# Column softmax turned on VectorE and through DRAM, and the last stage in written order

## Chip, cores and metric

One NeuronCore of a Trainium2 chip runs the whole program. The metric is the device time of one execution in microseconds (us). Engines are called TensorE (PE), VectorE (DVE), ScalarE (ACT), GpSimd (POOL) and the sync engine (SP), which issues nearly all DMAs.

## What is computed

Three layers, one after the other, all in float32. Every matmul of the big layers is made of three passes over a high and a low part of each operand (hi·hi, hi·lo, lo·hi), so operands are split all the time: the high part by a ScalarE copy, the low part by a VectorE subtraction.

```
# x: 8 batches, 8 heads, 512 tokens, 64;  state: 8, 8, 32 rows, 64
a     = softmax_over_rows(scale * x @ state.T)          # per token
xread = a @ state
a2    = softmax_over_tokens(scale * state @ x.T)        # per state row ("columns")
sread = a2 @ x
X = concat([xread, sread], tokens) -> 8 * (512 + 32) tokens of 512
Y = relu(X @ w1_in)**2 @ w1_out                         # 512 -> 2048 -> 512
h = Y @ w2_in                                           # 512 -> 1024
s = h * softmax(h);  ln = (s - mean) / sqrt(var + 1e-6) * g
out = ln @ w2_out                                       # 1024 -> 512
```

## The kernel before

**First layer and attention.** The list `items` holds one step for each batch b and each 128 wide chunk f of the hidden layer, 16 steps a batch; batch 8 stands for the 256 tokens read into the states (sread of all batches). A step (`step`, L1337) computes the hidden chunk f with 6 long matmuls (12 for batch 8), squares it (`square`: ScalarE relu to r, VectorE r times the PSUM bank, called r below; `high` and `low` split the square into gh and gl), and projects the chunk f-2 back to 512 columns with 12 matmuls into four accumulators (`project`). After the last chunk the accumulators are evicted to ev_x, half by ScalarE and half by VectorE, and stored (x_d). The PSUM pool of the hidden chunks has two buffers, so r of a step must be done before the hidden matmuls of the next step but one.

The attention of batch b runs spread over 15 steps (0 to 14) beside the steps of the batch before: attention step k lies in step k+2 of that batch, and 14 in step 0 of batch b itself. For batches from 2 on, `attention` returns for each k four lists: work ahead of the hidden matmuls (`tensor`), on ScalarE, on VectorE, and `after` the hidden matmuls; only the first VectorE part stands ahead of gl, and the r multiply comes after all of them. x arrives in a layout for 32x32 block turns (`load_xq`, four quarters of xbuf), is turned on VectorE in k = 0 to 3 (`turn_x`), and arrives a second time by tokens in the same buffer (`load_half`) for sread. The scores st have (4 heads x 32 rows) on partitions and 512 tokens along. The row softmax turns them on VectorE, goes over rows and turns back (`back`, k = 10 and 12). The column softmax goes along the tokens (`col_max`, `col_exp`, `col_norm`, done at k = 8 and 10), and then st must have tokens on partitions: TensorE transposes it in blocks of four into a PSUM bank (`col_ps`, L747, k = 11 and 12), ScalarE copies that to e2 (`col_copy`), and `sread` (L616) multiplies it with x in two halves of 32 small instructions, ahead of the hidden matmuls of k = 13 and 14.

**Second layer.** Tokens are taken in 17 pairs of 128-token tiles, A and B. Each pair's h comes from seven products by Strassen's scheme (`product`, 6 matmuls each, `post` for the adds on VectorE and ScalarE); product i of pair q is slot n = 7q + i (`slot`, L1433). Beside the products a slot carries the SoLU and layer norm of earlier pairs (sol_max, sol_exp, sol_mul, sol_square, sol_var with a pow on GpSimd, sol_norm), the turn of ln on VectorE and through DRAM (`turn`, `fetch_ln`), its split (`part_hi`, `part_lo` to lh and ll), the load, sums and splits of later pairs (`load_pair`, `sums` on GpSimd, `pair_hi`, `pair_lo`), and a number of steps ("flows", 3 matmuls each, 272 in all) of the down projection `down`, which takes ll and lh of one tile after the other. The last pair is turned on TensorE (`by_pe`). Slots 0 to 11 lie in steps 5 to 15 of batch 8, slot 12 and 13 between the last projections. `prepare` (L1167) loads and splits the second layer's weights in the steps of batches 7 and 8, and the first two pairs.

**What sets the order.** Engines run their queues in order. Inside `tc.manual_schedule` the order on TensorE, VectorE, ScalarE and SP is as the code writes it; GpSimd's is always planned. Up to step 28 a table of hand (PLAN) is walked through, then written steps run to the end of batch 6. From batch 7 on to slot 13 a planner with its own costs orders the instructions, and from slot 14 on the order is written again:

```
    for s in range(steady.stop, len(items)):      # batches 7 and 8: planned
        ...prepare(b, f); step(s, b, f); slots 0 to 11
    ...split_down(2); slot(12, 0); ...split_down(3); slot(13, 0)
    with tc.manual_schedule(engines=by_hand):
        for n in range(14, 7 * NPAIR):
            slot(n, {14: 0, 15: 2, 16: 1, 17: 1}.get(n, 2 if n < 32 else (2, 3, 2, 2, 3, 2, 2)[n % 7]))
        for n in range(7 * NPAIR, 7 * NPAIR + 14):
            slot(n, 3)
```

Of the kernel before, what the change touches and what calls it, by code (L numbers as in the profile page):

```python
# [20 lines left out]
def memory_attention_relu2_solu(  # L21
# [16 lines left out]
    P = 128  # L38
# [29 lines left out]
    ]  # L68
    x2p_d = [dram.tile([P, NM, S], F32, name=f"x2p_d{b}", tag=f"x2p_{b}") for b in range(2)]
# [433 lines left out]
    def attention(b):  # L503
# [111 lines left out]

        def sread(half):  # L616
# [137 lines left out]

        def col_max(q):
# [16 lines left out]
        def at(f, *a):  # L772
# [4 lines left out]
            11: [(col_ps, 0)], 12: [(col_ps, 1)], 13: [(sread, 0)], 14: [(sread, 1), (sread_out,)],  # L777
# [12 lines left out]
            11: [(a_high, 0), (col_copy, 0)],  # L790
# [18 lines left out]
        after = {12: [(col_copy, 1)]}  # L809
# [357 lines left out]
    def prepare(b, f):  # L1167
# [27 lines left out]
        elif f == 4:  # L1195
            split_block("T2", "T2", *halves_of(w_tile("w2")))
            pair_hi(0, 1)
            pair_lo(0, 1)
        elif f == 5:
            minus("T4", "R21", "T2", "R11")  # L1200
            load_pair(1)
        elif f == 6:
            split_block("B21", "R21", *halves_of(w_tile("w2")))
            pair_hi(1, 0)
            pair_lo(1, 0)
        elif f == 7:
            sums(1)
# [6 lines left out]
        if f in (12, 14):  # L1214
            split_down(f // 2 - 6)
# [121 lines left out]
    def step(s, b, f):  # L1337
# [65 lines left out]
        rest()  # L1403
        squares.append((b, f, n, r, True))
# [11 lines left out]
        if ws == 15 and 1 <= w < B - 2:  # L1416
            load_xq(w + 2, 0)
# [14 lines left out]

    def slot(n, flows):  # L1433
        q, i = divmod(n, 7)
        work = []

        def at(p, f, *a):
            if 0 <= p < NPAIR:
                work.append(lambda: f(p, *a))

        last = NPAIR - 1
        if i == 0:
            if q == 2:
                at(0, part_hi, "A")
                at(0, part_lo, "A")
            at(q - 1, sol_exp, "B")
            at(q - 1, sol_mul, "A")
        elif i == 1:
            at(q - 1, sol_square, "A")
            if 0 < q - 2 != last:  # L1450
                at(q - 2, part_hi, "A")
            at(q - 1, sol_mul, "B")
        elif i == 2:
# [4 lines left out]
            if 0 < q - 2 != last:  # L1458
                at(q - 2, part_lo, "A")
        elif i == 3:  # L1460
            at(q - 1, sol_norm, "A")
            at(q - 1, sol_var, "B")
        elif i == 4:
            at(q - 1, sol_norm, "B")
            if q - 2 != last:
# [3 lines left out]
        elif i == 5:  # L1469
            if q - 1 < last:  # L1470
                at(q - 1, fetch_ln, "A")
            if q - 2 in (0, last - 1):
                at(q - 2, part_lo, "B")
            if q - 1 < last:
                at(q - 1, turn, "B")
        elif i == 6:
# [5 lines left out]
            if 0 < q - 2 < last - 1:  # L1482
                at(q - 2, part_lo, "B")
        if q < NPAIR:
# [5 lines left out]
        if i == 5:  # L1490
            at(q, sol_max, "A")
            at(q + 2, sums)
        elif i == 6:
            at(q, sol_max, "B")
            at(q + 2, pair_hi, 0)
        elif i == 0:
            if q > 0:
                at(q + 1, pair_lo, 0)
        elif i == 1:
            at(q + 2, load_pair)  # L1500
        elif i == 2:
            at(q + 1, pair_hi, 1)
        elif i == 3:
            at(q + 1, pair_lo, 1)
        for w in work:
# [4 lines left out]
    steady = range(7 * FPC, (B - 1) * NF)  # L1510
    with tc.manual_schedule(engines=by_hand):
        for s in steady:
            step(s, *items[s])
    for s in range(steady.stop, len(items)):
        b, f = items[s]
        if (b, f) > (B - 1, 0):
            prepare(b, f)
        step(s, b, f)
        if b == B and f >= 5:
            for n in {13: (8, 9), 14: (10,), 15: (11,)}.get(f, (f - 5,)):  # L1520
                slot(n, 0)
        if (b, f) == (B - 1, 0):
            sa.close()
            pools["x"] = pool("xp", 2, side="right")
            pools["w"] = pool("wx", 2, side="right")
            pools["p"] = pool("pp", 2, side="right")
            pools["s"] = pool("sp", 4, side="right")
            ps_2[0] = pool("ps_2a", 1, space=PSUM, side="right")

    pend.append(low(*high(*squares.pop(0))))  # L1530
    for m in range(4):
        run(project(*pend[0], m))
    split_down(2)
    slot(12, 0)
    for m in range(4):
        run(project(*pend[1], m))
    sb.close()
    ps_2[1] = pool("ps_2b", 1, space=PSUM)
    pools["t"] = pool("ps_t", 1, space=PSUM)
    pools["o"] = pool("ps_o", 2, space=PSUM)  # L1540
    split_down(3)
    slot(13, 0)
    with tc.manual_schedule(engines=by_hand):
        for n in range(14, 7 * NPAIR):
            slot(n, {14: 0, 15: 2, 16: 1, 17: 1}.get(n, 2 if n < 32 else (2, 3, 2, 2, 3, 2, 2)[n % 7]))
        for n in range(7 * NPAIR, 7 * NPAIR + 14):
# [31 lines left out]
```

## Time and profile before

| | |
|---|---|
| median of 3 runs | 1045.85 us (1044.44 to 1046.21) |
| the profiled execution's own time | 1045.91 us |
| its span, first to last instruction | 1044.1 us |
| TensorE busy, matmuls | 1021.6 us, 98% |
| VectorE busy | 779.0 us, 75% |
| ScalarE busy | 632.6 us, 61% |
| GpSimd busy | 146.3 us, 14% |
| granted TensorE clock | 1.00 in every slice |
| HBM traffic | 165 GB/s over the span |

The profile is of one execution. A timeline row gives the start, the duration, engine and source line, the tile written and the tiles read, and in brackets how long the engine sat idle before it and what released it. Matmuls overlap: a long matmul (512 columns) has a duration of 0.39 us and the next one starts 0.23 us later, so what an instruction costs TensorE is read from start to start. Tiles have the names of the code without numbers; xs is xbuf, ps_c the bank of the transposes, ps_sr that of sread, ps_h that of the hidden chunk, acc the accumulators, b the products' banks.

### The profile page before, as it was taken

To read this page: it belongs to the slowest core of one execution; us is meant where nothing else is said; L and a number is where in the kernel's file an instruction comes from. 1 tells how busy PE (TensorE), PEld (TensorE's weight loads), DVE (VectorE), ACT (ScalarE), POOL (GpSimd) and SP (SyncE) were. 2 spreads that over 40 slices of the span, in tenths; PEclk is the share of its full clock that TensorE was granted. 3 is DMA by queue.
4 is the path that set the end of the run, shared out by engine and by line. 5 is a ranking of instruction groups with operands and counts; after the bars stand their busy time and mean duration, and the time that the engine had idled before them with its cause. 6 is when DMAs were issued, how large, how long until landed. Compare 5 with 4: busy or idle time off the path is not lost.

```text
span 1044.1 us, 14955 instructions
## 1 busy us (share of the span) xinstructions
PE 1021.6 (98%) x5142; PEld 844.4 (81%) x5142; DVE 779.0 (75%) x1367; ACT 632.6 (61%) x1063; POOL 146.3 (14%) x174
## 2 busy tenths in 40 slices
PE   6899999999999999999999999999999999999998
PEld 5588788888888888888888887997888888888877
DVE  7999899787577588697785555578878777877861
ACT  6897786466566565465564434366756665665562
POOL 1300000000000000000000102222332332233110
PEclk9999999999999999999999999999999999999999
DMA  9788788686587494533441315533544534444431
GB/s 276 228 281 249 257 280 259 190 228 197 138 242 218 128 270 141 129 94 84 121 119 46 127 61 153 190 122 121 172 151 163 170 132 165 167 143 151 142 131 51
DMA packets 182956, 174.54 MB, mean 167 GB/s; under 512 B 98784, under 2 KB 132832, under 8 KB 182880
## 3 DMA queue, kind: packets, MB, share of 16 engines
q1 hardware_dynamic: 182160, 173.33, 54.1%
q8 instruction: 40, 0.66, 0.3%
q14 instruction: 36, 0.29, 0.1%
q10 hardware_dynamic: 720, 0.26, 0.1%
HBM read 106.43 MB, written 66.06 MB: 165 GB/s over the span
## 4 chain that ended last, share of the span: by engine, by line
PE 88%; DVE 5%; DMA 3%; ACT 2%; issue 1%; POOL 1%; ACTq 0%; SPq 0%; DVEq 0%; POOLq 0%
PE b L986 14%; PE acc L147 11%; PE acc L148 11%; PE acc L149 11%; PE ps_h L147 6%; PE ps_h L149 6%; PE ps_h L148 6%; PE ps_o L1129 5%; PE ps_o L1128 5%; PE ps_o L1127 5%; PE ps_sr L628 2%; DMA w1i_d<-w1in 1%; DMA st_x<-x_d 1%; PE ps_sw L399 1%; PE ps_sw L400 1%
## 5 line engine op out<-in xcount | busy, mean ns | idle before, releaser
L147 PE MATMUL acc<-gh,w1out 128*128 128x512 f32 (+1 forms) x576 | 218.6, 379 | 1.2 <-DVE ev_x L872 1.2
L148 PE MATMUL acc<-gl,w1out 128*128 128x512 f32 (+1 forms) x576 | 217.5, 378 | 0.4 <-DVE gl L843 0.4
L149 PE MATMUL acc<-gh,w1out 128*128 128x512 f32 (+1 forms) x576 | 217.6, 378 | 0.0
L828 ACT ACTIVATE r<-ps_h 128x512 f32<-128x512 f32 (+1 forms) x144 | 82.4, 573 | 122.4 <-PE ps_h L149 118.9
L843 DVE TENSOR_TENSOR gl<-r,gh 128x512 fp32r<-128x512 f32 (+1 forms) x144 | 97.7, 679 | 59.5 <-ACT gh L838 53.9
L838 ACT ACTIVATE gh<-r 128x512 fp32r<-128x512 f32 (+1 forms) x144 | 87.2, 606 | 71.2 <-DVE r L832 70.0
L147 PEld LDWEIGHTS acc<-gh,w1out 128*128 128x128 f32 x576 | 108.4, 188 | 21.7 <-DVE ev_x L872 1.6
L832 DVE TENSOR_TENSOR r<-r,ps_h 128x512 f32<-128x512 f32 (+1 forms) x120 | 77.6, 647 | 64.4 <-ACT r L828 63.6
L148 PEld LDWEIGHTS acc<-gl,w1out 128*128 128x128 f32 x576 | 108.4, 188 | 20.7 <-DVE gl L843 0.8
L149 PEld LDWEIGHTS acc<-gh,w1out 128*128 128x128 f32 x576 | 108.4, 188 | 20.2
L1129 PE MATMUL ps_o<-w,ll 128*128 128x512 f32 x272 | 106.2, 391 | 1.1 <-DVE ll L1108 1.1
L1127 PE MATMUL ps_o<-w,lh 128*128 128x512 f32 x272 | 106.1, 390 | 0.2 <-ACT lh L1102 0.2
L1128 PE MATMUL ps_o<-w,lh 128*128 128x512 f32 x272 | 105.9, 389 | 0.0
L147 PE MATMUL ps_h<-ah,sw 128*128 128x512 f32 x256 | 102.5, 400 | 0.0
L149 PE MATMUL ps_h<-ah,sw 128*128 128x512 f32 x256 | 99.9, 390 | 0.0
L148 PE MATMUL ps_h<-al,sw 128*128 128x512 f32 x256 | 99.9, 390 | 0.0
L207 POOL TENSOR_TENSOR cw<-cw,ce 128x512 f32<-128x512 f32 x16 | 20.7, 1296 | 483.1 <-DVE ce L204 417.3
L986 PE MATMUL b<-w,x2h 128*128 128x512 f32 x272 | 84.1, 390 | 0.3 <-DVE hB L1004 0.3
L1059 POOL TENSOR_TENSOR var<-var,mhalf 128x1 f32<-128x1 f32 x34 | 44.6, 1311 | 235.8 <-DVE var L1058 235.5
L1129 PEld LDWEIGHTS ps_o<-w,ll 128*128 128x128 f32 x272 | 51.0, 188 | 13.0 <-DVE ll L1108 2.6
L1038 ACT ACTIVATE e<-hA,nm 128x1024 f32<-128x1024 f32 x17 | 19.6, 1151 | 67.2 <-DVE nm L1033 67.2
L1127 PEld LDWEIGHTS ps_o<-w,lh 128*128 128x128 f32 x272 | 51.1, 188 | 11.0 <-ACT lh L1102 0.6
(233 smaller groups left out, 2067.8 us busy)
## 6 DMA issues: line engine op xcount, KB each, us to landing
ln_d<-ln_sq SPq DMA_DIRECT2D x32, 512.0 KB, 3.2
ln_t<-ln_d SPq DMA_DIRECT2D x128, 128.0 KB, 2.8
stg<-sw_d SPq DMA_DIRECT2D x120, 128.0 KB, 3.3
sw_d<-ev_sw SPq DMA_DIRECT2D x28, 512.0 KB, 3.4
st<-in_moe_w_out_dram SPq DMA_DIRECT2D x24, 512.0 KB, 5.2
st_x<-x_d SPq DMA_DIRECT2D x34, 256.0 KB, 3.8
w1i_d<-w1in SPq DMA_DIRECT2D x16, 512.0 KB, 5.5
st<-in_moe_w_in_dram SPq DMA_DIRECT2D x16, 512.0 KB, 5.5
```

The source lines that it names most:

```text
L147: nc.tensor.matmul(out=ps, lhsT=lh, rhs=rh, start=first and i == 0, stop=False)
L148: nc.tensor.matmul(out=ps, lhsT=lh, rhs=rl, start=False, stop=False)
L149: nc.tensor.matmul(out=ps, lhsT=ll, rhs=rh, start=False, stop=last and i == n - 1)
L828: nc.scalar.activation(out=r, in_=ps, func=AF.Relu)
L832: nc.vector.tensor_tensor(out=r, in0=r, in1=ps, op=ALU.mult)
L838: nc.scalar.activation(out=gh, in_=r, func=AF.Copy if times else AF.Square)
L843: nc.vector.tensor_tensor(out=gl, in0=r, in1=gh.bitcast(F32), op=ALU.subtract)
L986: nc.tensor.matmul(out=ps, lhsT=l, rhs=r, start=first and k == 0 and j == 0, stop=k == 1 and j == 2, skip_group_check=True,)
L1059: nc.gpsimd.tensor_tensor(out=var, in0=var, in1=mhalf, op=ALU.pow)
L1127: nc.tensor.matmul(out=ps, lhsT=a, rhs=wt[:, 0, o : o + 512], start=(k == 0), stop=False)
L1128: nc.tensor.matmul(out=ps, lhsT=a, rhs=wt[:, 1, o : o + 512], start=False, stop=False)
L1129: nc.tensor.matmul(out=ps, lhsT=bb, rhs=wt[:, 0, o : o + 512], start=False, stop=(k == NK - 1))
```

## The change

Part one, attention from batch 3 on: `col_ps` and `col_copy` go. Instead VectorE turns st in 32x32 blocks into sq (k = 10 and 11), SP writes sq to a DRAM tile (256 KB) and, in `after` of k = 11 and 12, reads it back in four pieces of 64 KB into e2, now by heads; `sread` picks its columns accordingly. For all batches from 2 on both halves of sread stand together, behind the hidden matmuls of k = 14. The four loads of the next x move from the end of step 15 and the starts of steps 0, 1, 2 to the end of step 0, start and end of step 1, and start of step 2.

Part two: batches 7 and 8 and slots 0 to 13 also stand inside `manual_schedule`; `prepare` is called inside the step, behind r. A table EARLY gives the side work of slots 5 to 19 and 22 (first list: its first entry stands ahead of `post`, the rest behind; second list: behind those). The flows start at slot 14 instead of 15, some mid slots have one less, and 16 tail slots follow instead of 14. Some work of `prepare` moves by a step.

```diff
+    st_d = [dram.tile([P, 2, S], F32, name=f"st_d{b}", tag=f"st{b}") for b in range(2, B)]
...
+        def col_of(t, h):
+            if b < 3:
+                return v["e2", t // 2][:, t % 2, h * NS : (h + 1) * NS]
+            return v["e2", h // 4][:, h % 4, t * NS : (t + 1) * NS]
...
-                            rhs=v["e2", t // 2][:, t % 2, h * NS : (h + 1) * NS],
+                            rhs=col_of(t, h),
...
+        def col_turn(q):
+            sq = atp.tile([P, S], F32, tag="st", name="sq", bufs=4)
+            nc.vector.transpose(
+                out=sq.rearrange("p (j t n) -> p t j n", j=4, t=NT),
+                in_=v["st", q].rearrange("p (t j n) -> p t j n", j=4, t=NT),
+            )
+            nc.sync.dma_start(out=st_d[b - 2][:, q, :], in_=sq)
+
+        def col_fetch(q):
+            e = v["e2", q] = atp.tile([P, 4, NT * NS], F32, tag="e", name="e2")
+            at = st_d[b - 2][:, q, :].rearrange("(g r) (j c) -> j r g c", g=4, j=4)
+            for k in range(4):
+                nc.sync.dma_start(out=e[32 * k : 32 * (k + 1)], in_=at[k])
...
-            11: [(col_ps, 0)], 12: [(col_ps, 1)], 13: [(sread, 0)], 14: [(sread, 1), (sread_out,)],
...
-        after = {12: [(col_copy, 1)]}
+        after = {14: [(sread, 0), (sread, 1), (sread_out,)]}
+        if b == 2:
+            tensor |= {11: [(col_ps, 0)], 12: [(col_ps, 1)]}
+            scalar[11].append((col_copy, 0))
+            after[12] = [(col_copy, 1)]
+        else:
+            vector[10].append((col_turn, 0))
+            vector[11].append((col_turn, 1))
+            after |= {11: [(col_fetch, 0)], 12: [(col_fetch, 1)]}
...
-            pair_lo(0, 1)
-        elif f == 5:
             minus("T4", "R21", "T2", "R11")
             load_pair(1)
+        elif f == 5:
+            pair_lo(0, 1)
         elif f == 6:
+            sums(1)
             split_block("B21", "R21", *halves_of(w_tile("w2")))
...
-        if f in (12, 14):
-            split_down(f // 2 - 6)
+        if f in (13, 14):
+            split_down(f - 13)
...
-            if ws in (0, 1, 2):
-                load_xq(w + 1, ws + 1)
+            if ws in (1, 2):
+                load_xq(w + 1, 2 * ws - 1)
...
+        if (b, f) > (B - 1, 0):
+            prepare(b, f)
         squares.append((b, f, n, r, True))
...
-        if ws == 15 and 1 <= w < B - 2:
-            load_xq(w + 2, 0)
+        if ws in (0, 1) and 2 <= w < B - 1:
+            load_xq(w + 1, 2 * ws)
...
+    EARLY = {
+        5: ([], [(sol_max, 0, "A"), (sums, 2), (sol_exp, 0, "A")]),
+        6: ([(sol_mul, 0, "A")], [(sol_square, 0, "A"), (sol_max, 0, "B"), (pair_hi, 2, 0)]),
+        7: ([(sol_exp, 0, "B"), (sol_var, 0, "A")], [(sol_mul, 0, "B"), (pair_lo, 2, 0)]),
+        8: ([(sol_norm, 0, "A"), (sol_square, 0, "B")], [(turn, 0, "A"), (load_pair, 3)]),
+        9: ([(sol_var, 0, "B")], [(pair_hi, 2, 1), (fetch_ln, 0, "A"), (pair_lo, 2, 1)]),
+        10: ([(sol_norm, 0, "B")], [(turn, 0, "B")]),
+        11: ([(fetch_ln, 0, "B")], [(split_down, 2)]),
+        12: ([], [(sol_max, 1, "A"), (sums, 3)]),
+        13: ([(sol_exp, 1, "A"), (part_hi, 0, "A")], [(part_lo, 0, "A"), (sol_max, 1, "B"), (pair_hi, 3, 0), (split_down, 3)]),
+        14: ([], [(sol_mul, 1, "A"), (sol_exp, 1, "B"), (part_hi, 0, "B"), (sol_square, 1, "A"), (pair_lo, 3, 0)]),
+        15: ([(sol_mul, 1, "B")], [(sol_var, 1, "A"), (sol_square, 1, "B"), (part_lo, 0, "B"), (load_pair, 4)]),
+        16: ([(sol_norm, 1, "A")], [(sol_var, 1, "B"), (pair_hi, 3, 1), (turn, 1, "A")]),
+        17: ([], [(sol_norm, 1, "B"), (pair_lo, 3, 1)]),
+        18: ([(fetch_ln, 1, "A")], [(turn, 1, "B")]),
+        19: ([], [(sol_max, 2, "A"), (sums, 4)]),
+        22: ([(sol_square, 2, "A")], [(part_hi, 1, "A"), (part_lo, 1, "A"), (sol_mul, 2, "B"), (load_pair, 5)]),
+    }
...
+        if n in EARLY:
+            work, then = ([lambda f=f, a=a: f(*a) for f, *a in l] for l in EARLY[n])
+        elif i == 0:
+            if q == NPAIR:
+                at(q - 2, part_hi, "A")
...
+            if q == NPAIR:
+                at(q - 2, part_lo, "A")
...
+    with tc.manual_schedule(engines=by_hand):
+        for s in range(7 * FPC, len(items)):
...
+        slot(12, 0)
...
+        for n in range(13, 7 * NPAIR):
+            slot(n, 0 if n < 14 else 1 if n in (18, 22) else 2 if n < 32 or n < 75 and n % 7 == 4 else (2, 3, 2, 2, 3, 2, 2)[n % 7])
+        for n in range(7 * NPAIR, 7 * NPAIR + 16):
             slot(n, 3)
```

## Rows read from the trace of the kernel before

**Rows 1.** The page's part 1: busy us (share of the span) and instructions of each engine.

```profile
PE 1021.6 (98%) x5142; PEld 844.4 (81%) x5142; DVE 779.0 (75%) x1367; ACT 632.6 (61%) x1063; POOL 146.3 (14%) x174
```

**Rows 2.** Windows: length, busy us of PE, PEld, DVE, ACT, POOL, clock, DMA share, GB/s.

```profile
423.00:494.00 71.00, 71.00 (x371) 58.46 (x370) 54.08 (x96) 39.03 (x70) 4.74 (x4) 1.00 0.39 109
626.00:656.00 30.00, 27.52 (x175) 24.68 (x174) 16.47 (x22) 12.14 (x22) 8.91 (x9) 1.00 0.55 174
```

**Rows 3.** TensorE timeline at a ps_c: start us, us, what, count.

```profile
485.65 0.39 PE L149 MATMUL acc<-gh,w1out 128*128 128x512 f32 x1
485.88 0.60 PE L558 MATMUL ps_c<-ident,st 128*128 128x128 f32 x4
...
486.55 0.40 PE L148 MATMUL ps_h<-al,sw 128*128 128x512 f32 x1
```

**Rows 4.** TensorE timeline at the sread blocks of batch 0 and of batch 6.

```profile
70.32 0.40 PE L149 MATMUL acc<-gh,w1out 128*128 128x512 f32 x1
70.65 2.06 PE L628 MATMUL ps_sr<-e,xs 128*64 128x32 f32 x64
...
72.97 0.39 PE L148 MATMUL acc<-gl,w1out 128*128 128x512 f32 x1
...
490.23 0.39 PE L149 MATMUL acc<-gh,w1out 128*128 128x512 f32 x1
490.54 1.13 PE L628 MATMUL ps_sr<-e,xs 128*64 128x32 f32 x32
...
491.93 0.39 PE L148 MATMUL ps_h<-al,sw 128*128 128x512 f32 x1
```

**Rows 5.** VectorE timeline, attention steps 11 and 12; in brackets idle us before, releaser.

```profile
484.03 0.69 DVE L832 TENSOR_TENSOR r<-r,ps_h 128x512 f32<-128x512 f32 x1 [0.51 <-ACT r L828]
484.63 0.70 DVE L737 STREAM_TRANSPOSE at<-e 128x512 f32<-128x512 f32 x1
...
488.60 0.69 DVE L832 TENSOR_TENSOR r<-r,ps_h 128x512 f32<-128x512 f32 x1 [1.29 <-ACT r L828]
```

**Rows 6.** DMA issues: out<-in, queue, count, KB each, median us to landing.

```profile
ln_d<-ln_sq SPq DMA_DIRECT2D x32, 512.0 KB, 3.2
ln_t<-ln_d SPq DMA_DIRECT2D x128, 128.0 KB, 2.8
...
xs<-in_x_dram SPq DMA_DIRECT2D x96, 64.0 KB, 3.0
```

**Rows 7.** Sync engine's timeline at the loads of x.

```profile
491.48 4.59 SPq L498 DMA_DIRECT2D xs<-in_x_dram  x8
```

**Rows 8.** TensorE's waits from 600 us on: total us, times, longest us.

```profile
PE ps_h L147 <- DVE r L832: 1.3, 1, 1.3
PE acc L147 <- DVE ev_x L872: 1.2, 2, 0.8
PE ps_o L1129 <- DVE ll L1108: 1.1, 3, 0.5
PE b L986 <- DVE hB L1004: 0.3, 1, 0.3
PE ps_o L1127 <- ACT lh L1102: 0.2, 1, 0.2
```

**Rows 9.** TensorE timeline at one wait in the states' steps.

```profile
648.82 0.28 PE L149 MATMUL acc<-gh,w1out 128*128 128x256 f32 x1
650.38 0.39 PE L147 MATMUL ps_h<-sh,w1in 128*128 128x256 f32 x1 [1.28 <-DVE r L832]
650.60 0.28 PE L148 MATMUL ps_h<-sl,w1in 128*128 128x256 f32 x1
```

**Rows 10.** VectorE timeline in the states' steps.

```profile
642.04 1.23 DVE L970 TENSOR_TENSOR x2l<-st_s,x2h 128x1024 fp32r<-128x1024 f32 x1 [1.72 <-ACT x2h L966]
```

**Rows 11.** Groups by line: busy us, mean ns of one, idle before and releaser.

```profile
L1108 DVE TENSOR_TENSOR ll<-ln_t,lh 128x1024 fp32r<-128x1024 f32 x32 | 39.0, 1219 | 4.0 <-DMA out_dram<-ob 3.5 <-ACT lh L1102 0.4
...
L1045 DVE SCALAR_TENSOR_TENSOR e<-e,s,hA 128x1024 f32<-128x1024 f32 x17 | 22.0, 1292 | 0.6
```

More of the change, by code (lines that the diff above doesn't have):

```diff
@@ L789, in attention @@
             10: [(col_norm, 1)],
[L790 removed]
+            11: [(a_high, 0)],
             13: [(a_high, 1)],
@@ L1446, in slot @@
             at(q - 1, sol_exp, "B")
             at(q - 1, sol_mul, "A")
+            at(q + 1, pair_lo, 0, into=then)
         elif i == 1:
             at(q - 1, sol_square, "A")
-            if 0 < q - 2 != last:
+            if q == NPAIR:
+                at(q - 2, part_lo, "A")
+            elif q - 2 != last:
                 at(q - 2, part_hi, "A")
             at(q - 1, sol_mul, "B")
+            at(q + 2, load_pair, into=then)
         elif i == 2:
@@ L1457, in slot @@
             at(q - 1, sol_var, "A")
-            if 0 < q - 2 != last:
+            if 1 < q - 2 < last - 1:
                 at(q - 2, part_lo, "A")
+            at(q + 1, pair_hi, 1, into=then)
         elif i == 3:
@@ L1462, in slot @@
             at(q - 1, sol_var, "B")
+            at(q + 1, pair_lo, 1, into=then)
         elif i == 4:
             at(q - 1, sol_norm, "B")
-            if q - 2 != last:
+            if 0 < q - 2 != last:
                 at(q - 2, part_hi, "B")
@@ L1475, in slot @@
                 at(q - 1, turn, "B")
+            at(q, sol_max, "A", into=then)
+            at(q + 2, sums, into=then)
         elif i == 6:
@@ L1481, in slot @@
             at(q, sol_exp, "A")
-            if 0 < q - 2 < last - 1:
+            if 1 < q - 2 < last - 1:
                 at(q - 2, part_lo, "B")
+            at(q, sol_max, "B", into=then)
+            at(q + 2, pair_hi, 0, into=then)
+        if n == 0:
+            then.clear()
         if q < NPAIR:
@@ L1489, in slot @@
             post(q, i)
[L1490 to L1505, printed above, removed]
+        for w in work + then:
             w()
@@ L1508, in slot @@
             down_k()
-    steady = range(7 * FPC, (B - 1) * NF)
-    with tc.manual_schedule(engines=by_hand):
[L1512 to L1546, printed above, removed]
+    def last_pools():
+        sa.close()
+        for k, name, bufs in (("x", "xp", 2), ("w", "wx", 2), ("p", "pp", 2), ("s", "sp", 4)):
+            pools[k] = pool(name, bufs, side="right")
+        ps_2[0] = pool("ps_2a", 1, space=PSUM, side="right")
@@ new lines, in memory_attention_relu2_solu @@
+    with tc.manual_schedule(engines=by_hand):
+        for s in range(7 * FPC, len(items)):
+            b, f = items[s]
+            step(s, b, f)
+            if b == B and f >= 5:
+                for n in {13: (8, 9), 14: (10,), 15: (11,)}.get(f, (f - 5,)):
+                    slot(n, 0)
+            if (b, f) == (B - 1, 0):
+                last_pools()
+        pend.append(low(*high(*squares.pop(0))))
+        for m in range(4):
+            run(project(*pend[0], m))
+        slot(12, 0)
+        for m in range(4):
+            run(project(*pend[1], m))
+        sb.close()
+        ps_2[1] = pool("ps_2b", 1, space=PSUM)
+        pools["t"] = pool("ps_t", 1, space=PSUM)
+        pools["o"] = pool("ps_o", 2, space=PSUM)
+        for n in range(13, 7 * NPAIR):
+            slot(n, 0 if n < 14 else 1 if n in (18, 22) else 2 if n < 32 or n < 75 and n % 7 == 4 else (2, 3, 2, 2, 3, 2, 2)[n % 7])
+        for n in range(7 * NPAIR, 7 * NPAIR + 16):
```

14 lines of the change are left out of this document (4 added, 10 removed).

## The prediction

> **What bounds the kernel.** I read the page first, then the windows by stage, TensorE's waits, and the timeline where something moves. TensorE is busy for 1021.6 of 1044.1 us [rows 1]. In a stretch of the attention batches it is busy for all of 71 us, at full clock, while VectorE has 54 and ScalarE 39 [rows 2]. So in that stage only what leaves TensorE's own queue shortens the run. Around the tokens of the states it is busy for 27.52 of 30 us [rows 2]: 2.5 us are lost there to waits, and further single waits follow down to the tail [rows 8]. The profiled execution took 1045.91 us, 1.8 more than its span, and the median of the runs is 1045.85, so 1045.9 is the base.
>
> **Part one: column softmax turned on VectorE.** A long matmul in full flow starts 0.227 us after the one before. In [rows 3] the last matmul before the turn starts at 485.65 and the second after it at 486.55: 0.90 us for two long matmuls and four 128x128 transposes, so the four cost 0.90 - 0.45 = 0.45 us. Batches 3 to 7 lose two such blocks each: 10 x 0.45 = **4.5 us off TensorE**. This is issue to issue, with the refilling of the pipeline in it. The bounds are nothing (were another engine to end the step) and the block's whole 0.60 us [rows 3], 6.0 in all; I take the steps between starts, since TensorE has no idle time there. The Trainium skill (TensorE: Matmul & The Clock Gate, Part 4: PE-mode transpose) gives about 275 ns for a transpose inside a kernel; by that price 40 of them would be 11 us and the new time an estimated 6.5 us lower than mine. The trace does not bear that out as a loss, at 0.45 us for four.
>
> The reads of x (sread) also move, from ahead of the hidden matmuls of steps 13 and 14 to one block behind those of step 14. In [rows 4] a block of 32 stands between 490.23 and 491.93: 1.70 - 0.45 = 1.25 us. A block of 64 (batch 0) stands between 70.32 and 72.97: 2.65 - 0.45 = 2.20 us. Two of 32 cost 2.50, one of 64 costs 2.20: entering and leaving is paid once, 0.30 us a batch, in batches 2 to 7 **1.8 us**.
>
> What is added: on VectorE two transposes of 128x512 a batch. The nearest row has 0.70 us; the strided output may cost up to twice that, and less than 0.70 isn't plausible for the same elements. I take 0.70. They stand in attention steps 10 and 11, ahead of that step's r multiply. There VectorE sat idle 0.51 us before r, and 1.29 us before the r of step 12 [rows 5]. So r comes at most about 1 us later, and the surplus is gone in step 12. A step is 18 x 0.227 = 4.1 us, and r frees a PSUM buffer that TensorE wants again in the next step but one, 4 us or more later. Cost: nothing; without that cover, 0.7 us a step, 7 us in all. ScalarE loses ten copies, which gains nothing, as it is idle a third of the time and more.
>
> The round trip: the second turn ends with step 11. Its write is 256 KB; the rows give 3.2 us for twice that and 2.8 us for a 128 KB read back [rows 6]; the reads here are 64 KB in four pieces. An issue takes SP 4.59 / 8 = 0.57 us with small packets [rows 7]. That makes about 3.2 + 2.8 + 3 x 0.57 = 7.7 us after the turn. The second piece also takes the buffer that the turn back at 484.63 [rows 5] frees, in step 12, which is earlier than its data. TensorE comes to sread two steps and six matmuls later, 2 x 4.1 + 1.4 = 9.6 us. So about 2 us of cover, and a step more for the first piece. The new wait of TensorE, on landings where it was on two copies, has the twelve projections of the step behind it and all later work; I take it at 0, with up to 3 us a batch if landings double. On SP the reads wait for the write; behind them stand only weight loads for a chunk that is a step or more away.
>
> The loads of the next x move past sread as well, in pairs around steps 0 to 2 of the batch; the last two now also stand behind the stores of x2 in step 1. The first is issued when sread ends, 1.4 + 2.2 = 3.6 us into step 0, and takes four issues and 3.0 us [rows 6, 7]: it has landed at 3.6 + 2.3 + 3.0 = 8.9 us. VectorE wants it for step 2, once the r of step 1 is through: 4.1 + 2.2 for step 0 and some 2.5 more, 8.8 us. Cost 0; if it is late by 1 us, VectorE slips by that and catches up, as it has 54 us of work in 71 [rows 2].
>
> **Part two: written order from the last batch on.** TensorE's order is the same as the planner's by the code; VectorE's and ScalarE's differ. In the first three steps of the states' tokens (2.9 us each) the planner put two pairs' splits: an x2l of 1.23 us, after 1.72 of waiting for its x2h, holds up the r and the evictions queued behind it [rows 10]. TensorE waits for ev_x 1.2 us in two waits and for r 1.3 us [rows 8]. Each restart costs more than its idle time: between 648.82 and 650.60 stand 1.78 us where two short matmuls take 0.24, that is 1.54 for a wait booked at 1.28, 0.26 more [rows 9]. So the loss is 2.5 + 3 x 0.26 = 3.3 us. In the written order the second pair's splits come in steps 6 and 7 and in slots 2 and 3, and the first pair's in steps 3 to 5, where its load, which now starts after t3l, has some 8 us to land. Evictions and r are then alone: **3.3 us gained**. If the load is late, ScalarE stands in pair_hi and half of it is lost.
>
> Slots 13 to 19 stay crowded. VectorE has in slots 13 to 15 two adds and a pair_lo (0.7 to 1.0 each), two sol_mul (1.28 and three small ones, 1.9 each), two part_lo of 1.22, a split and a maximum of about as much [rows 11]: some 11 us, against 6.9 us of TensorE there. The first down projection also begins at slot 14, one earlier. Placing these by hand, I get TensorE waiting about 1.1 us for ll in slot 14 and 1.0 us in slot 19 for the add of v, which stands behind a chain of square, pow, norm and turn: with restarts 2.3 us or a little more. Before, the waits of that stretch are 0.6 us of ll (two of three) and 0.3 for hB, with restarts 1.7 [rows 8]. So **0.6 us given back**; from a gain of 1.7 to a loss of 4 (VectorE's whole surplus).
>
> Tail: 46 of 272 steps of the down projection are left at the last product instead of 41, so the second-last pair's first tile is wanted 3.4 us later, and its split is written one slot earlier. The waits of 0.5 (the third ll) and 0.2 us (lh) [rows 8] go: 0.7 + 2 x 0.26 = **1.2 us**.
>
> **Sum:** 4.5 + 1.8 + 3.3 - 0.6 + 1.2 = 10.2 us. 1045.9 - 10.2 = **1035.7 us**.
>
> **Rivals.**
> 1. The written order gives back all that it takes: VectorE's surplus of 4 us in slots 13 to 15 falls on TensorE. For: the same work, in-order queues, pow on GpSimd inside the chain. Against: none of it was ever worth over 1.7 us before. Time: 1045.9 - 6.3 = 1039.6, and 1041.5 if a bit more is lost.
> 2. Slower: sread waits for the round trip. If write and read land in twice the rows' time (6.4 and 5.6), the second piece comes at 12.0 + 1.7 = 13.7 us against 9.6: 4.1 us in each of five batches, 20.5 us, and the time is 1056. It decides from 2.5 us a batch on (5 x 2.5 = 12.5 eats the 10.2 and leaves 2.1); 2 us a batch end within the measurement. For: four more DMA waits in a row, and SP issues in order behind them. Against: in this stage queues are lightly used, and medians of 2.8 to 3.2 come from busier stages. The Trainium skill (VectorE: DVE Perf Modes, Rules for kernel authors) would also leave a 128x128 transpose on TensorE where PSUM will do; by that rule the change loses, while the rows say that TensorE is the one engine with no time.
> 3. The x loads come late for the turn in step 2 and VectorE's slip reaches TensorE: 1 us in each of five batches, 1040.7.
>
> **How the numbers follow.** The forecast has 0.62, with 1033 to 1038.5 as its own range (late slots from +1.7 to -2, the loads of pair one). Rival 1 has 0.22, rival 2 0.12 (half of it slower, half within the measurement), rival 3 0.04. About 0.2%, 2.1 us, is what can be told from no change. Faster 0.62 + 0.22 + 0.04 = 0.88, same 0.06, slower 0.06. The range 1032.5 to 1041.5 takes in the forecast and rivals 1 and 3; left out are rival 2 and a little at the edges.
>
> **What would show it.** Steps of batches 4 to 7: TensorE still without idle time, no ps_c, a batch 1.2 us shorter (0.9 + 0.3); sread as one block with no DMA ahead of it as its releaser. The states' first steps: no wait for ev_x or r; if one stands there for x2h, pair_hi was late. Slots 13 to 19: waits for ll and for v of 1 us each. The second-last pair in the tail: no wait for lh. It is wrong if a wait of sread on st_d shows, or if TensorE's sum of waits after the last batch is over 5 us.

## The result, and the profile after

The changed kernel takes 1033.59 us, median of 4 runs (1032.50 to 1034.19); the kernel before took 1045.14 beside it. The ratio is 0.9893, 95% interval 0.9879 to 0.9907: 11.5 us faster, where 10.2 were forecast (1035.7). The profiled execution took 1034.19 us with a span of 1032.3, 11.7 and 11.8 less than before.

The page's part 1, of the changed kernel (answers [rows 1]):

```profile
PE 1011.4 (98%) x5102; PEld 840.3 (81%) x5102; DVE 785.3 (76%) x1377; ACT 626.7 (61%) x1053; POOL 140.5 (14%) x174
```

Forty transposes have left TensorE, ten copies ScalarE; ten transposes have come to VectorE. TensorE is still busy for 98%: it is shorter because it has less to issue and fewer waits. The windows of the same two stretches (columns as in [rows 2]):

```profile
420.00:491.00 71.00, 71.00 (x420) 59.10 (x420) 56.32 (x99) 38.51 (x68) 3.90 (x3) 1.00 0.45 127
614.00:644.00 30.00, 30.00 (x188) 27.17 (x187) 16.50 (x23) 13.25 (x24) 10.71 (x8) 1.00 0.45 151
```

In the attention stretch TensorE has no idle time, as before; VectorE has 2.2 us more to do. Around the tokens of the states the 2.5 us that were lost are gone. The read block on TensorE's timeline (answers [rows 4]):

```profile
488.92 0.39 PE L150 MATMUL ps_h<-ah,sw 128*128 128x512 f32 x1
489.24 2.06 PE L634 MATMUL ps_sr<-e,xs 128*64 128x32 f32 x64
491.23 0.50 PE L148 MATMUL acc<-gh,w1out 128*128 128x512 f32 x1
491.56 0.39 PE L149 MATMUL acc<-gl,w1out 128*128 128x512 f32 x1
```

It is one block of 64 with no wait in brackets. From 488.92 to 491.56, less two long matmuls, it costs 2.64 - 0.45 = 2.19 us. For the round trip ahead of it, the view of the tile st_d gives the issues with their counts, and the landing times of all fifty DMAs:

```profile
L773 SPq DMA_DIRECT2D e<-st_d x40: 309/430/973, 262.2 to 551.0; - x40
L767 SPq DMA_DIRECT2D st_d<-sq x10: 319/334/528, 257.1 to 547.3; - x10
...
DMA to landing us min/median/max: 1.8/2.1/5.1
```

The median is 2.1 us, where the forecast took 3.2 and 2.8 from larger DMAs of other stages [rows 6]. In batch 6 VectorE's second turn and SyncE's second read back stand here:

```profile
476.82 0.70 DVE L763 STREAM_TRANSPOSE sq<-st 128x512 f32<-128x512 f32 x1
```

```profile
480.44 1.74 SPq L773 DMA_DIRECT2D e<-st_d  x4
```

TensorE's waits from 600 us on (answers [rows 8]):

```profile
PE b L1013 <- DVE v L1031: 1.7, 1, 1.7
PE ps_o L1156 <- DVE ll L1135: 0.5, 1, 0.5
PE ps_o L1154 <- ACT lh L1129: 0.3, 1, 0.3
```

The waits for ev_x, for r, and those of the tail are gone. One is new and larger than any before: 1.7 us for v (in slot 19; u, v and hB are the adds of `post` that empty a product's bank). The other two stand in slot 14.

Where the gain comes from is read by a ruler: the start of the n-th matmul of a kind (hidden chunk, product, down projection) in the kernel before, less its start in the other kernel. The growth of that lead over a stage is what the stage gained, with the refilling of the pipeline in it. The late slots end at 785 us, where both kernels have done the same number of steps of the down projection. A column names the kernel that is held against the one before; the experiments below say what it is.

| stage (us in the kernel before) | changed | part one alone | read block alone | part two alone | changed, with unused transposes |
|---|---|---|---|---|---|
| up to 178 | 0.58 | 1.26 | 0.97 | 0.50 | 1.48 |
| read of batch 2, to 217 | 0.35 | 0.35 | 0.35 | 0.00 | 0.35 |
| batch 3, to 294 | 1.66 | 1.66 | 0.67 | 0.00 | 0.67 |
| batch 4, to 390 | 1.84 | 1.72 | -0.61 | 0.21 | 0.64 |
| batches 5, 6, 7, each | 1.33 | 1.33 | 0.35 | 0.00 | 0.35 |
| states' tokens, 633 to 666 | 3.27 | -0.56 | -0.04 | 3.27 | 3.27 |
| last hidden chunks, to 699 | 0.29 | 0.01 | 0.01 | 0.29 | 0.29 |
| late slots, to 785 | -1.70 | 0.10 | 0.13 | -1.73 | -1.71 |
| middle and tail | 1.33 | 0.00 | 0.03 | 1.33 | 1.33 |
| all | 11.61 | 8.54 | 2.55 | 3.87 | 7.36 |

Up to 178 us no line has changed, and all the kernels run for this study gain 0.5 to 1.8 us there: the profiled execution of before was late in that place. So 11.0 of the 11.6 us are the change's.

### The profile page after: what moved, and what is told of

It is laid out like the page before. It is cut to its first block, busy times and chain, and to the rows that moved or that the text cites. A ratio compares the mean times of both kernels' runs of the same rounds, so it can differ in the third digit from the quotient of the medians.

```text
span 1032.3 us, 14956 instructions
## 1 busy us (share of the span) xinstructions
PE 1011.4 (98%) x5102; PEld 840.3 (81%) x5102; DVE 785.3 (76%) x1377; ACT 626.7 (61%) x1053; POOL 140.5 (14%) x174
## 4 chain that ended last, share of the span: by engine, by line
PE 91%; issue 2%; DMA 2%; DVE 2%; ACT 2%; SPq 1%; POOL 0%; ACTq 0%; DVEq 0%; POOLq 0%
PE b L1013 14%; PE acc L148 12%; PE acc L149 12%; PE acc L150 12%; PE ps_h L148 6%; PE ps_h L149 6%; PE ps_h L150 6%; PE ps_o L1156 6%; PE ps_o L1155 6%; PE ps_o L1154 6%; PE ps_sr L634 2%; PE ps_sw L400 1%; PE ps_sw L401 1%; DMA st64w<-in_moe_w_in_dram 1%; DMA stg<-ev_sw 1%
## 5 line engine op out<-in xcount | busy, mean ns | idle before, releaser
L148 PE MATMUL ps_h<-ah,sw 128*128 128x512 f32 x256 | 100.2, 391 | 0.0
L150 PE MATMUL ps_h<-ah,sw 128*128 128x512 f32 x256 | 99.7, 389 | 0.0
L1086 POOL TENSOR_TENSOR var<-var,mhalf 128x1 f32<-128x1 f32 x34 | 34.1, 1003 | 251.2 <-DVE var L1085 251.2
L1129 ACT ACTIVATE lh<-ln_t 128x1024 fp32r<-128x1024 f32 x32 | 33.7, 1054 | 45.1 <-PE ps_o L1155 45.1
L1156 PEld LDWEIGHTS ps_o<-w,ll 128*128 128x128 f32 x272 | 51.0, 188 | 11.8 <-DVE ll L1135 1.3
L1013 PEld LDWEIGHTS b<-w,x2h 128*128 128x128 f32 x272 | 50.5, 188 | 12.3 <-DVE v L1031 2.1
```

Of the source, the lines that this page charges most:

```text
L148: nc.tensor.matmul(out=ps, lhsT=lh, rhs=rh, start=first and i == 0, stop=False)
L150: nc.tensor.matmul(out=ps, lhsT=ll, rhs=rh, start=False, stop=last and i == n - 1)
L1013: nc.tensor.matmul(out=ps, lhsT=l, rhs=r, start=first and k == 0 and j == 0, stop=k == 1 and j == 2, skip_group_check=True,)
L1086: nc.gpsimd.tensor_tensor(out=var, in0=var, in1=mhalf, op=ALU.pow)
L1156: nc.tensor.matmul(out=ps, lhsT=bb, rhs=wt[:, 0, o : o + 512], start=False, stop=(k == NK - 1))
```

## The experiments

Times are medians; ratios are to runs of the kernel before on the same chip.

**Part one alone** (batches 7 and 8 planned as before).

> Part one alone, batches 7 and 8 planned as before. Theory A (TensorE is full in the attention batches, so the time falls by the issue time that leaves its queue): the forecast's terms give 4.5 + 1.8 = 6.3 us; by the trace of the changed kernel, where batches 2 to 7 came out 7.8 us shorter, 6.3 to 7.8, so about 1038 against 1045.1, and the stretch from batch 8 on as long as before. Rival B (a page price of 275 ns for each of 40 transposes): 11 + 1.8 = 12.8 us, 1032. Rival C (the parts hold only together, as the planner delays the read block of batch 7): under 5 us.

Measured: 1036.95 us, before 1045.06; ratio 0.9921 (0.9908 to 0.9933), 8.1 us. By the table batches 2 to 7 gain 7.7 us, near theory A's upper end. The planned steps of the states lose 0.6: their wait for r is 2.1 us here, against 1.3 before. Rival B is out by 5 us, and the gain is well over the 5 us of rival C.

**Part two alone.**

> Part two alone, attention as before. Theory A (the two parts are separate, each pays at its own place): 3.3 us gained in the first steps of the states' tokens, 1.7 lost in slots 13 to 19, 1.2 gained in the tail, with 0.3 between: about 3.1 us, 1042. Rival (the written order pays only because part one took ten copies and turns off ScalarE and TensorE near the last batch): under 1.5 us. Waits of TensorE for ll in slot 14 and for v in slot 19 of 0.8 and 1.7 us stand here too by theory A.

Measured: 1041.95 us; ratio 0.9969 (0.9957 to 0.9980), 3.1 us. From the states' tokens on it has the numbers of the changed kernel stage by stage, its loss included, with this wait of TensorE:

```profile
PE b L986 <- DVE v L1004: 1.7, 1, 1.7
...
```

8.1 + 3.1 = 11.2 us against 11.5: the parts add up within the noise, and neither needs the other.

**The read block alone**, with the moved x loads (their lines are left out here):

```diff
-            11: [(col_ps, 0)], 12: [(col_ps, 1)], 13: [(sread, 0)], 14: [(sread, 1), (sread_out,)],
+            11: [(col_ps, 0)], 12: [(col_ps, 1)],
...
-        after = {12: [(col_copy, 1)]}
+        after = {12: [(col_copy, 1)], 14: [(sread, 0), (sread, 1), (sread_out,)]}
```

> Only the read of x in one block behind the hidden matmuls of step 14, and the moved x loads; the transposes stay on TensorE and the copies on ScalarE in all batches. Theory A (entering and leaving a block is paid once): 0.30 us a batch, 1.8 us in six batches, 1043.3; each batch 0.3 us shorter. Rival B (the small waits of 0.1 to 0.2 us of TensorE that are gone in batches 3 and 4 of the changed kernel came from the place of the read block and not from the transposes): 2.6 to 3 us, with these waits gone here. Rival C (a block is only moved): 0.

Measured: 1042.64 us, ratio 0.9978 (0.9968 to 0.9988), 2.4 us. Theory A holds with 0.35 instead of 0.30 us a batch, and rival B in part beside it: batch 3 gains a second third of a microsecond from the block's place alone. Batch 4 gains the same in the kernel with unused transposes (0.64); its -0.61 here is one wait. TensorE's timeline, then ScalarE's, of this kernel:

```profile
379.59 0.50 PE L684 MATMUL ps_s<-xh,bd 128*128 128x512 f32 x1 [1.20 <-ACT ev_sw L401]
```

```profile
378.42 0.63 ACT L445 ACTIVATE sw<-stg 128x512 fp32r<-128x512 f32 x1 [3.02 <-DMA stg<-sw_d]
378.96 1.07 ACT L401 ACTIVATE ev_sw<-ps_sw 128x512 f32<-128x512 f32 x2
```

ScalarE waits for a chunk of weights, the evictions queue behind it, and TensorE wants their bank. Before, ScalarE stood 1.73 us at that place, 1.13 in the changed kernel, and no such wait reached TensorE. It need not be the edit: the changed kernel has such a wait in its second profile, below, and none in its first.

**Transposes put back on TensorE for nobody**, in batches 3 to 7 of the changed kernel:

```diff
+        def unused(tp):
+            ps = bank("ps_u")
+            for t in range(4):
+                nc.tensor.transpose(ps[:, t * P : (t + 1) * P], ident, ident)
...
+            tensor |= {11: [(unused, 0)], 12: [(unused, 1)]}
```

> The changed kernel with two blocks of four 128x128 transposes of a constant put back on TensorE in each of batches 3 to 7, at the place where the removed ones stood; nobody reads them, so there is no copy and the softmax still goes through VectorE and DRAM. Theory A (what was gained is TensorE's issue time, 0.45 us a block): 4.5 us slower than the changed kernel, 1038.1. Rival B (275 ns a transpose): 11 us slower, 1044.6. Rival C (the gain was ScalarE's ten copies and the banks that they held): no slower, 1033.6.

Measured: 1039.04 us, ratio 0.9941 (0.9929 to 0.9953), some 5 us slower than the changed kernel (0.9893). By the table batches 3, 5, 6 and 7 lose 0.98 us each (1.33 - 0.35), 0.49 a block, and batch 4 loses 1.20: theory A. One of the ten on TensorE's timeline:

```profile
482.17 0.39 PE L150 MATMUL acc<-gh,w1out 128*128 128x512 f32 x1
482.40 0.60 PE L760 MATMUL ps_u<-ident 128*128 128x128 f32 x4
482.75 0.48 PE L148 MATMUL ps_h<-ah,sw 128*128 128x512 f32 x1
483.07 0.40 PE L149 MATMUL ps_h<-al,sw 128*128 128x512 f32 x1
```

There is no copy and no reader here, and the price is whole again: it is TensorE's issue time and nothing of ScalarE's copies. The Trainium skill (TensorE: Matmul & The Clock Gate, Part 4: PE-mode transpose) gives about 275 ns as the duration of one bf16 transpose; four of them added up would be an estimated 1.1 us a block. As a price the trace does not bear that out: the four f32 transposes overlap, last 0.60 us together and cost 0.49.

**The way through DRAM made longer** for the second half of the columns, by one copy and by three:

```diff
+            for to in hop_d[b - 2] if q else []:
+                nc.sync.dma_start(out=to, in_=src)
+                src = to
```

> The changed kernel, but the second half of the turned columns takes one more way through DRAM in each of batches 3 to 7: it is copied to another DRAM tile (256 KB, one issue) before it is read back. Such a copy takes what a write took, 2.1 us to land, and 0.3 to 0.5 to issue: some 2.6 us later. Theory A (the cover that the trace of the changed kernel shows, from the landing of the second half at 484.2 us to the read block at 489.24, is 5 us): no loss, 1033.7. Rival B (the cover is the 2 us of the forecast): 0.6 us and more in each of five batches, 1037 and over, with TensorE waiting for the landing.

> As the one above with three copies in a row, some 7.8 us later. Theory A (5 us of cover): 2.8 us lost in each of five batches, and a restart of 0.3 each, 15.5 us: 1049, slower than the kernel before, with waits of TensorE's read block for the landing and nowhere else. Rival B (2 us of cover): 5.8 us and the restart in each, 30 us, 1064. Rival C (the landings of a batch are late in any case only in the first, and later batches shift): under 5 us.

Measured with one copy: 1034.24 us, ratio 0.9892 (0.9875 to 0.9908), no loss. SyncE's timeline and the read block:

```profile
479.68 0.50 SPq L776 DMA_DIRECT2D hop_d<-st_d  x1
483.63 1.73 SPq L780 DMA_DIRECT2D e<-hop_d  x4
```

```profile
488.53 2.06 PE L637 MATMUL ps_sr<-e,xs 128*64 128x32 f32 x64
```

The second half is asked for 4.9 us ahead of the block, against 8.8 in the changed kernel (480.44 to 489.24). That is 3.9 us later, and TensorE does not wait. With three copies: 1058.7 us, ratio 1.0127 (1.0112 to 1.0142), 25 us slower than the changed kernel, between theory A and rival B. TensorE's waits, its timeline in batch 6, and windows in batches 6, 4 and 5:

```profile
PE ps_sr L637 <- DMA e<-hop_d: 13.4, 5, 3.8
...
```

```profile
502.93 1.12 PE L637 MATMUL ps_sr<-e,xs 128*64 128x32 f32 x32
507.01 1.12 PE L637 MATMUL ps_sr<-e,xs 128*64 128x32 f32 x32 [2.96 <-DMA e<-hop_d]
```

```profile
505.00:507.00 2.00, 0.00 (x0) 0.00 (x0) 0.00 (x0) 0.00 (x0) 0.00 (x0) 1.00 0.39 114
...
508.50:511.20 2.70, 2.70 (x8) 2.02 (x8) 1.03 (x2) 0.48 (x1) 0.00 (x0) 0.50 0.79 219
```

```profile
362.00:364.70 2.70, 2.70 (x8) 2.12 (x7) 0.12 (x1) 0.00 (x0) 0.00 (x0) 0.50 0.65 205
```

```profile
435.00:437.00 2.00, 2.00 (x27) 1.73 (x24) 0.53 (x1) 0.80 (x2) 0.00 (x0) 1.00 0.93 314
```

SyncE asks for the second half at 503.75, 0.8 us behind the start of the block: 9.6 us later than in the changed kernel. TensorE waits 2.96 for it, so the cover is about 6.7 us, more than theory A's 5: half a block runs meanwhile. Yet the loss is 24 us by the same ruler, and the idle time only 13.4. The rest is the clock. After four of the five waits the granted clock of the next matmuls is 0.50, the 1.2 GHz level, and each starts 0.43 us after the last instead of 0.23. In batch 6 this lasts 3.4 us; in batches 3, 4 and 7, whose waits ended at 277.46, 358.64 and 580.37, it lasts 5.4 to 6.3 us behind the wait. Together that is 21.2 us at half pace, which costs 10.6: what was missing. After the fifth wait, of 1.7 us in batch 5, the clock stayed at 1.00, and that batch lost 1.85 us where the others lost 4.7 to 6.5.

**The late slots, and batch 2.** One entry of the written order moved (the turn behind the add of v); then also no down projection in slot 14; then also batch 2 by part one's way (no run has batch 2's edit alone).

```diff
-        16: (..., [(sol_var, 1, "B"), (pair_hi, 3, 1), (turn, 1, "A")]),
-        17: ([], [(sol_norm, 1, "B"), (pair_lo, 3, 1)]),
+        16: (..., [(sol_var, 1, "B"), (pair_hi, 3, 1)]),
+        17: ([], [(turn, 1, "A"), (sol_norm, 1, "B"), (pair_lo, 3, 1)]),
```

> The changed kernel once more, beside the three below: 1033.6, as before. If the two parts only add up, its gain is the 8.1 of part one alone and the 3.1 of part two alone: 11.2 us below the kernel before.

> The changed kernel with one entry of the side work moved: the turn of the second pair's first tile goes from the end of slot 16 to slot 17 behind the add of v. Theory A (TensorE's 1.7 us in slot 19 are the turn and what it waits for, a chain of square, pow and norm with VectorE's queue shut behind it): the wait for v is gone, 1.5 to 2 us faster than the changed kernel, 1031.8; the turn itself comes no later than norm allows. Rival B (VectorE has more work than time in slots 13 to 19, so the wait only moves to the next one who needs it): under 0.5 us, with a wait for ll, hB or lh in slots 19 to 23 in its place.

> As the one above, and slot 14 carries no step of the down projection, which leaves 48 instead of 46 steps behind the last product. Theory A (lh and ll of the first tile come about 0.9 us too late for slot 14, and one slot later they are there): TensorE's waits of 0.3 and 0.5 us with their restarts go, 1.3 us more, 1030.5 and no wait for lh or ll left ahead of slot 19. Rival B (the work is taken from slot 14 but the tail gets it, where the last pair's splits hold TensorE up): under 0.4 us more.

> As the one above, and batch 2 takes the way of part one too (turned on VectorE and through DRAM, two blocks of four transposes less). Theory A (TensorE is the full engine there as well, and VectorE, 88% busy in that stage, still gets r done in the next step): 0.9 to 1.0 us more, 1029.6. Rival B (VectorE is so full beside batch 1 that two turns of 0.70 us push r past the point where TensorE wants its bank): 0 to 2 us slower than without, with waits of ps_h for r near step 11 of that attention.

Measured: the changed kernel 1033.72 (ratio 0.9889, 0.9876 to 0.9903); turn moved 1033.43 (0.9885, 0.9872 to 0.9899); slot 14 emptied 1035.45 (0.9908, 0.9895 to 0.9922); batch 2 as well 1041.56 (0.9964, 0.9951 to 0.9978). The second profile of the changed kernel repeats the table within 0.1 us, but for the stretch up to 178 us and for batch 4's stage, where it has 0.54 instead of 1.84. There ScalarE waits for a late chunk of weights, and then TensorE for ScalarE:

```profile
299.79 0.63 ACT L446 ACTIVATE sw<-stg 128x512 fp32r<-128x512 f32 x1 [2.84 <-DMA stg<-sw_d]
```

```profile
300.96 0.51 PE L690 MATMUL ps_s<-xh,bd 128*128 128x512 f32 x1 [1.02 <-ACT ev_sw L402]
```

With the turn moved, rival B holds: the wait for v is gone, two of 0.5 us stand in its place (for hB, and one put down to s), and the late slots gain 0.2.

```profile
PE ps_o L1156 <- DVE s L1069: 0.5, 1, 0.5
...
PE b L1013 <- DVE hB L1031: 0.5, 1, 0.5
...
```

With slot 14 emptied both expectations miss: 2 us slower. TensorE comes earlier to the same adds and waits longer (0.8 for u, 2.0 for hB), so two steps taken out, 1.4 us of work, gained nothing there; in the tail these steps cost that time, and 0.8 beside it. The clock adds to the loss. Windows around the wait for hB, of this kernel and then of the one with batch 2, whose late slots are the same code:

```profile
709.50:712.00 2.50, 0.48 (x3) 0.08 (x1) 2.25 (x4) 2.17 (x3) 0.51 (x2) 1.00 0.51 210
712.30:715.40 3.10, 3.10 (x9) 2.42 (x8) 3.03 (x5) 0.26 (x1) 0.00 (x0) 0.51 0.51 155
```

```profile
717.00:719.20 2.20, 0.63 (x3) 0.19 (x1) 1.95 (x3) 2.10 (x3) 0.75 (x2) 1.00 0.39 162
719.50:722.00 2.50, 2.33 (x10) 1.95 (x11) 2.47 (x4) 0.00 (x1) 0.00 (x0) 1.00 0.20 64
```

A wait of 2.02 us was followed by the half clock in the one, a wait of 2.04 in the other was not; their late slots differ by 1.5 us.

Batch 2 by part one's way fits neither theory. The waits are for DMAs, and of rival B only 0.6 us shows (a wait for gh at 188.90, behind the r that follows the turn). TensorE's timeline, VectorE's second turn, SyncE's timeline, and a window:

```profile
198.90 1.12 PE L634 MATMUL ps_sr<-e,xs 128*64 128x32 f32 x32 [1.56 <-DMA e<-st_d]
202.10 1.37 PE L634 MATMUL ps_sr<-e,xs 128*64 128x32 f32 x32 [2.08 <-DMA e<-st_d]
```

```profile
186.87 0.70 DVE L763 STREAM_TRANSPOSE sq<-st 128x512 f32<-128x512 f32 x1
```

```profile
189.37 0.33 SPq L171 DMA_DIRECT2D st<-in_moe_w_in_dram  x1
...
190.94 0.42 SPq L767 DMA_DIRECT2D st_d<-sq  x1
191.46 1.91 SPq L773 DMA_DIRECT2D e<-st_d  x4
193.41 0.91 SPq L903 DMA_DIRECT2D x_d<-ev_x  x2
197.93 0.32 SPq L773 DMA_DIRECT2D e<-st_d  x1
```

```profile
194.00:197.00 3.00, 3.00 (x15) 2.44 (x13) 2.49 (x4) 0.93 (x3) 0.00 (x0) 1.00 0.99 358
```

Two things are late. SyncE's queue stands 5.0 us behind a load of weights, which waits for VectorE's eviction to ev_x and goes out at 189.37. So the second write leaves at 190.94, 3.4 us after its turn ended at 187.57, and the first read back leaves 3.8 us after its write had landed at 187.64. Then the second write takes 6.9 us to land: its read back is issued 7.0 us after it, where the changed kernel has 2.9 in batch 6 (477.55 to 480.44). The DMA engines are 99% busy there, with two stores of 512 KB behind the write. The stage loses 5.1 us where it gained 0.35; after the second wait the granted clock was at 0.50 for 3.4 us. This is the forecast's rival 2.

Full DMA engines alone did not do this: in the changed kernel batch 3's round trip meets them as well and costs TensorE no wait, though its two writes took 5.1 and 3.6 us. The window there (a packet counts where it starts, so the share can pass 1):

```profile
260.00:263.00 3.00, 3.00 (x15) 2.49 (x14) 1.86 (x4) 1.83 (x4) 0.00 (x0) 1.00 1.03 319
```

Its second write left 0.03 us after its turn. From the times above, an estimate: with the landings as they were but no delay in SyncE's queue, batch 2's halves would be there at 195.0 and 198.6, where TensorE came for them at 197.3 and about 198.5. No run parts the two causes. The Trainium skill's advice to leave a 128x128 transpose on TensorE where PSUM will do (VectorE: DVE Perf Modes, Rules for kernel authors) would have been right for this batch in this order, and cost about 1 us in each of the five others.

**Adds first.** The turn moved as above, pair_lo of slot 17 behind the add of hB in slot 18, part_hi of slot 22 ahead of the square:

```diff
+        17: ([], [(turn, 1, "A"), (sol_norm, 1, "B")]),
+        18: ([(fetch_ln, 1, "A")], [(pair_lo, 3, 1), (turn, 1, "B")]),
...
+        22: ([(part_hi, 1, "A"), (sol_square, 2, "A")], [(part_lo, 1, "A"), ...
```

> The changed kernel with three entries of the side work moved: the turn of the second pair's first tile behind the add of v in slot 17, the split pair_lo of slot 17 behind the add of hB in slot 18, and the ScalarE half of the first split of slot 22 ahead of the square. Theory A (what TensorE waits for in slots 17 to 23 is the place in VectorE's and ScalarE's queues, not their sum of work; with the adds first, the waits of 0.5 for hB and 0.5 for ll that came in place of the 1.7 for v go as well, each with a restart of 0.26): 1.5 us faster than with the turn moved alone, 1031.9. Rival B (VectorE's sum of work holds the stretch, and each move only hands the wait on): within 0.4 us of 1033.4, with other waits in place of these.

Measured: 1032.24 us, ratio 0.9875 (0.9860 to 0.9890); the late slots lose 0.2 instead of 1.7. Theory A holds for hB; the wait at the split that slot 22 makes stayed (0.4, put down to s). The last kernel puts slot 14's two steps into slot 15, and pair_lo of slot 21 behind ll:

> As the kernel with the three moved entries (1032.24), and two more: the two steps of the down projection of slot 14 go to slot 15 (four there) instead of to the tail, and the split of the fifth pair's first part in slot 21 goes behind the split of ll in slot 22. Theory A (the loss of the kernel that took the steps of slot 14 to the tail was the 1.4 us of work moved and a tail that was disturbed; the waits of slot 14, 0.3 and 0.5 us with restarts, are a matter of place): 1.0 us faster, 1031.2, no wait for lh or ll left in slots 14 to 23. Rival B (TensorE gets 1.2 us ahead and runs into VectorE's adds, which come when VectorE's chain of work lets them): within 0.4 us of 1032.2, with waits for u, v or hB in slots 16 to 19 of the same sum as those that went.

Measured: 1031.86 us, ratio 0.9870 (0.9853 to 0.9886). The median says rival B; by the ruler the late slots gain 0.4 more than in the kernel above (now +0.2, better than before the change). No wait for lh or ll is left, as theory A had it, but two of 0.3 have come, and the gain is less than half of its 1.0. TensorE's waits from 600 us on:

```profile
PE b L1013 <- DVE hB L1031: 0.3, 1, 0.3
PE b L1013 <- ACT s L1034: 0.3, 1, 0.3
```

This version has the lowest median and ratio of all. Its interval overlaps that of the changed kernel, so the 1.9 us between them rest on the ruler (1.70 + 0.19) more than on the medians.

## Why the prediction was right, point by point

- **TensorE is the full engine in the attention batches:** right, and shown: unused transposes put back took their issue time again, though ScalarE's copies stayed away.
- **Transposes 4.5 us:** 4.9, 0.49 a block instead of 0.45.
- **Read block 1.8 us:** 2.1, 0.35 a batch instead of 0.30. Left out: about 0.3 more in each of batches 3 and 4 from its place (batch 3 in the read block alone, batch 4 with unused transposes), 0.7 together. What the place frees there was not tested. Another 0.2 in batch 4 is not part one's, since part two alone gains it too.
- **Turns on VectorE at 0.70 us, no cost:** right; TensorE waits for no r in batches 3 to 7.
- **Round trip, 2 us of cover:** no wait came, as forecast, but the cover was mis-sized: about 6.7 us in batch 6. Most of that is distance. The second turn ended at 477.5, 11.7 us ahead of the block, where the forecast had it at the end of its step and 9.6: it stands ahead of r, and sixteen steps take 69.4 us (from block to block, 489.24 to 558.63), 4.3 each and not 4.1. The way itself took 7.0 us to the last landing at 484.6, against 7.7, and the second half is wanted half a block (1.1 us) later. Over batches 3 to 7 the distance was 11.3 to 13.4 us and the way 5.7 to 8.3.
- **Rival 2 (landings double):** it did not happen, but its mechanism is real: batch 2 shows it. That queues are lightly used, as the forecast held against it, is so in batches 5 to 7; around the round trips of batches 3 and 4 the DMA engines were about 80% busy and the writes took 3.1 to 5.1 us. (Its 12.5 less the 10.2 leaves 2.3, not 2.1; nothing hangs on it.)
- **Moved x loads, no cost:** right; no wait of TensorE came from them. Rival 3 did not happen.
- **States' tokens 3.3 us:** 3.27, in part two alone too. A gain of 0.29 in the last hidden chunks was not forecast.
- **Late slots -0.6 us:** -1.70, the term furthest off. The place was right (lh and ll in slot 14, v in slot 19). The changed kernel loses 1.35 and 1.97 us there with restarts, where the forecast had 2.3 together; it gave 1.0 us for v and no price for the chain of square, pow, norm and turn ahead of it. That chain passes through GpSimd:

```profile
706.18 1.46 POOL L1086 TENSOR_TENSOR var<-var,mhalf 128x1 f32<-128x1 f32 x1 [15.07 <-DVE var L1085]
...
707.61 0.74 POOL L979 TENSOR_TENSOR st_s<-st_x 128x256 f32<-128x256 f32 x1
...
708.31 0.19 POOL L1087 TENSOR_TENSOR bia<-var,mu 128x1 f32<-128x1 f32 x1
...
708.53 1.24 ACT L1092 ACTIVATE e<-e,bia,var 128x1024 f32<-128x1024 f32 x1 [1.75 <-POOL bia L1087]
...
709.80 1.25 DVE L1110 STREAM_TRANSPOSE ln_sq<-e 128x1024 f32<-128x1024 f32 x1 [2.51 <-ACT e L1092]
...
710.97 0.65 DVE L1031 TENSOR_TENSOR v<-b,s 128x512 f32<-128x512 f32 x1
```

This is the timeline of the changed kernel. The pow takes 1.46 us; a sum of another pair, 0.74, comes ahead of the small multiply that norm needs; VectorE then stands 2.51 us at the turn, with the add of v queued behind it. That GpSimd's part is what was missing is read from these rows, and no run takes it away. What the runs show is the place in the queue: with the turn behind v the wait for v is gone, and with the other adds first as well the late slots lose 0.2 instead of 1.7.

- **Tail 1.2 us:** 1.33.
- **Rival 1 (the written order gives back all):** wrong; it is worth 3.1 us alone.

By the ruler the sum missed by 1.4 us (11.6 against 10.2): transposes and read block +0.7, the unforeseen gain of batches 3 and 4 +0.9, tail +0.1, last chunks +0.3, the stretch before any change +0.6, late slots -1.1; the rounded terms add to 1.5. So the mechanisms were right, but that the sum came this close is partly luck, as errors of some 2 us and of -1.1 us met in it.

## What to carry to other kernels

Where one engine has no idle time in a stage, price an edit by the start-to-start time that leaves its queue, and prove it by putting the work back for nobody. A round trip through DRAM is free only as long as there is time between its start and its reader. The same edit that gains 1.3 us a batch lost 5.1 in batch 2, where the DMA engines were full and SyncE's queue stood behind another load. So read each stage's DMA share, and the order of the queue that issues, and not one stage's. In an in-order queue put what the full engine waits for ahead of what itself waits for a chain over other engines. Taking work from the full engine where it waits anyway gains nothing there.

## What the runs showed of the hardware

- A wait of TensorE can cost more than its length. After waits of 2.0 to 3.8 us (one in the kernel with slot 14 emptied, one with batch 2, four with three copies) the granted clock fell to 0.50, for 3.4 to 6.3 us behind the wait, and that cost some 1.5 to 3.0 us more. After 1.7 us it stayed at 1.00 each time (batch 5 with three copies, and v in the changed kernel and four others). Near 2 us it went either way: it also stayed at 1.00 after 2.04 us for hB with batch 2, and after the 2.11 us for r in part one alone, whose next window is this:

```profile
642.00:645.00 3.00, 3.00 (x25) 3.00 (x26) 1.61 (x4) 2.26 (x5) 0.00 (x0) 1.00 0.81 244
```

  Some 30 us into the program, where TensorE stands often, it fell for 3.4 us in seven of the fourteen profiles, behind waits of 1.3 us and less; in the kernel before it did not.
- A copy of 256 KB from DRAM to DRAM took 2.9 to 4.1 us to land in the kernels with copies, and SyncE's next issue stood behind it. In batches 5 to 7 of the same kernels a write of that size from SBUF landed in 2.0 to 2.1 us; in batches 3 and 4, with the DMA engines fuller, such writes took 3.2 to 5.3.
- In two executions of one kernel the same load of weights held ScalarE for 0.16 and 2.84 us, which cost batch 4's stage 1.3 us: a single profile does not settle a difference of that size.
